# Retention block and Strassen-like feed-forward on one core: a gate's erf moved back on ScalarE, and the sums of W_in spread differently over VectorE

## The chip, the core and the metric

The kernel runs on one core of a Trainium2 chip. The core has a matrix engine (TensorE, PE in the profile, whose weight loads are listed as PEld), an elementwise engine (VectorE, DVE), an activation engine (ScalarE, ACT), GpSimd (POOL) and a queue that issues transfers (SyncE, SP). Each works through its own instructions in order, and they wait for each other by semaphores. Matmul results land in PSUM banks, from which VectorE and ScalarE read. The metric is the device time of one execution in microseconds; less is better.

## The reference

```python
def _attn_ref(q, k, v):                     # (4, 8, 768, 64)
    state = np.zeros((B, H, D, D))
    for t in range(S):
        state = gamma * state + np.einsum('bhd,bhe->bhde', k[:, :, t], v[:, :, t])
        y[:, :, t] = scale * np.einsum('bhd,bhde->bhe', q[:, :, t], state)

def _moe_ref(x, w_in, w_out):               # x: 3072 x 512, d_ff = 2048
    h = x @ w_in
    sp = np.maximum(h, 0.0) + np.log1p(np.exp(-np.abs(h)))
    return (h * erf(sp)) @ w_out
```

The output y of the first becomes the rows of x. The second is a feed-forward layer whose activation is h times erf of softplus(h).

## The kernel before

**Tiling.** The 3072 rows are handled as 24 chunks of 128 of the retention part (j in the code). The first four chunks feed the first block of 512 rows; after that, 256 rows (two chunks) are handled at a time. The feed-forward part runs in groups g, each over a quarter (first block) or a half (later blocks) of the 2048 hidden columns. A group has four parts, which run on four engines and overlap with those of its neighbours:

- hidden: TensorE multiplies x by a piece of W_in, and ScalarE or VectorE takes the result out of PSUM into h;
- gate: ScalarE computes softplus(h), then erf of that, in place. Each of the two functions is preceded by a load of its table (ACT_TABLE_LOAD);
- gated (L890): VectorE multiplies h by the gate, in two halves;
- project: TensorE multiplies that by a piece of W_out. It runs one group later, so TensorE has hidden(g) to do while gate(g - 1) is made.

**The first block, g = 0 to 3.** Here hidden and project are plain matmuls (L901, L937). The input weights arrive as 64-bit words and are converted on the chip, 16 pieces in order: for the last eight of them ScalarE makes two scaled exponents of a piece (a pair of instructions on L366), and VectorE combines them with the words (L369, L370, L372, L375). Between these, retention work of the chunks j = 4 and 5 is put: `sub_begin` (scores and new state on TensorE), `sub_states` (VectorE: two masks on L676, then the state of L704 or L702), `sub_results` (TensorE, then two copies by ScalarE on L737) and `sub_sums` (VectorE, L746). The order on every engine is that of the program's text: a scheduler does not rearrange it. Conversion steps are drawn in by `pace`, by a running balance of estimated costs.

PSUM tiles come from small pools: two banks named hp, two named r, four named o. A new tile in a bank waits until the last reader of the old one is done.

**The later blocks, g = 4 and up.** Here hidden is a fast matrix multiplication (`hidden_steps`): 26 products, called steps, of sums of blocks of W_in (`W_SUMS`, 30 sums for each half s of W_in) with sums of blocks of x (`X_SUMS`). Each step is two matmuls into one of four banks (L992), in the order of the list `STEPS`:

```python
    (15, 10, 0, False, ((6, True),)),     # step 13: W 15, x 10, bank 0, one read
    (8, 9, 1, False, ((4, False),)),      # step 14: bank 1, one read
    (3, 4, 0, False, ()),                 # step 15: bank 0, no read
```

After a step, its bank is read and added to or subtracted from parts of h: by VectorE (L1004) where that part of h was written before, else by ScalarE (L1006, L1008). The next step in the same bank waits for that read. Banks 0 and 1 are the two of hp, 2 and 3 the two of r. Between steps the program puts other work by a table `order`, whose keys are step numbers: sums of W_in (L385), parts of `prepared(j + 1)` (L578, two of L587, two of L591: scaling and transposing the next chunk), and `last_steps`, sums of W_out's blocks (ScalarE L393, then a transfer that adds, issued by POOL on L394). From g = 5 on there are also three parts of the projection of the group before (`project_part`, L1075), after steps 14, 18 and 24.

The half s = 0 of W_in is used by even groups, s = 1 by odd ones. So the 30 sums of half 0 are due before or in g = 4, those of half 1 before or in g = 5; afterwards all sums are there.

After the steps of a group come softplus, `sub_visit` (the retention work of one chunk: matmuls on L777, L813, L792, L669, masks on L676, additions on L833 and L838), erf, projections and the gated product. For g = 4 the last two quarters of the projection of g = 3 (L937) and their copies out (`put_first`, L950) stand there.

The lines between the first block and the later groups, which the change rewrites, begin in the version before with 20 sums of half 0, `prepared(6)`, the x sums and the gated product of g = 3.

Of the kernel before, what the change touches and what calls it, by code (L numbers as in the profile page):

```python
# [18 lines left out]
AF = mybir.ActivationFunctionType  # L19
# [120 lines left out]
def kernel(  # L140
# [13 lines left out]
    nc = tc.nc  # L154
# [8 lines left out]
    TT = TCH // P  # L163
# [217 lines left out]
    def sum_in(s, upto):  # L381

        assert all(("hidden", 2 * FG + s * FG + u) in done for u in range(FG))
        for to, a, b, sign in W_SUMS[in_sums[s] : upto]:
            nc.vector.tensor_tensor(w_in_sb[:, s, to], w_in_sb[:, s, a], w_in_sb[:, s, b], op=OP[sign])  # L385
        in_sums[s] = max(in_sums[s], upto)
# [30 lines left out]
    last_steps = later_sums()  # L417
# [114 lines left out]
    idle = ps_o.tile([P, P], F32, name="o0")  # L532
# [41 lines left out]
    def prepared(j):  # L574

        if j >= NJ:
            return
        nc.vector.tensor_tensor(  # L578
            KQ[j][:, 0], KQ[j][:, 0],
            kq_s[:, j % NC, 0, :, None].to_broadcast([P, H, D]), op=ALU.mult,  # L580
        )
        yield
        blocks = (KB[j], KQ[j][:, 1].rearrange("p h d -> p (h d)"))
        for i, x in enumerate(blocks):
            x = x.rearrange("p (u a d) -> p u a d", u=HP, d=32)
            by = kq_b[:, j % NC, i, :, :, None].to_broadcast([P, HP, 4, 32])
            nc.vector.tensor_tensor(x, x, by, op=ALU.mult)  # L587
            yield
        for name, store, x in zip("kq", (KT, QT), blocks):
            store[j] = ret.tile([P, HP, C], F32, name=name + "T")  # L590
            nc.vector.transpose(store[j].rearrange("p u t -> p (u t)"), x)  # L591
            yield
# [156 lines left out]
    def sub_begin(j, pool=None):  # L749
        SC[j] = [ret_psum(pool) for _ in range(2)]  # L750
        sub_scores(j)
        sub_additions(j)
# [100 lines left out]
    def gate_softplus(g):  # L853


        name = "r" if g < 4 and g % 2 else "e"
        E[g] = act.tile([P, N], F32, name=name, bufs=1)
        nc.scalar.activation(E[g], HS[g], AF.Softplus)  # L858

    def gate(g):  # L860

        gate_softplus(g)
        if g:
            gate_erf(g)

    def gate_erf(g):

        for half in range(2) if g == NG - 1 else (slice(None),):
            if g == NG - 1:
                half = slice(half * N // 2, (half + 1) * N // 2)  # L870
            nc.scalar.activation(E[g][:, half], E[g][:, half], AF.Erf)  # L871
# [76 lines left out]
    def put_first(tt):  # L948
        o = E[G0 - 1].rearrange("p (u t c) -> p t u c", u=FG, t=TT)[:, tt]
        nc.scalar.copy(o, O[0][tt].rearrange("p (u c) -> p u c", u=FG))  # L950
        nc.sync.dma_start(out[tt * P : (tt + 1) * P, :].rearrange("p (u c) -> p u c", u=FG), o)

    G0 = n_ft // FG
# [29 lines left out]
    def hidden_steps(g):  # L983

        m, s = chunk_of(g), (g - G0) % 2
        HS[g] = act.tile([P, N], F32, name="h")
        banks = [pool.tile([P, FG, P], F32, name=name) for pool, name in ((ps_h, "hp"), (ps_r, "r")) for _ in range(2)]
        written = set()
        for w, x, bank, first, reads in STEPS:
            to = banks[bank]  # L990
            for u in range(2):
                nc.tensor.matmul(  # L992
                    to[:, u, :],
                    w_in_sb[:, s, w, u * P : (u + 1) * P],
                    XS[m](x),
                    start=first and u == 0,
                    stop=True,
                    skip_group_check=True,
                )
            of = to[:, :2].rearrange("p u t -> p (u t)")  # L1000
            for o, plus in reads:
                h = h_block(g, o)
                if o in written:
                    nc.vector.tensor_tensor(h, h, of, op=ALU.add if plus else ALU.subtract)  # L1004
                elif plus:
                    nc.scalar.copy(h, of)  # L1006
                else:
                    nc.scalar.activation(h, of, AF.Copy, scale=-1.0)  # L1008
                written.add(o)
            yield  # L1010
# [181 lines left out]
    for g in range(G0):  # L1192
        for u in range(FG):

            if g and u == (2 if g == 1 else 0):
                waiting.append((gated, g - 1))
            hidden(g, u)
            run(after[g][u][0])
            if (g, u) == (1, 0):
                room = 0.0  # L1200
            waiting.extend(after[g][u][1])
        gate(g)
        if g:
            for tt in range(TT):
                project(g - 1, tt)
                if g == 1 and tt < 2:
                    waiting.append((K_, 5) if tt else (sub_states, 4))
                elif g == 2 and tt == 0:
                    sub_results(4)
                    sub_begin(5, ps_h)  # L1210
                    waiting.append((sub_states, 5))
                elif g == 2 and tt == 1:
                    waiting.append((sub_sums, 4))

    def all_of(steps):
        for _ in steps:
            pass
# [6 lines left out]
    j = JPC + 2  # L1226
# [5 lines left out]
    next(last_steps)  # L1232
    project(G0 - 1, 0)
    put_first(0)
    sub_begin(j)
    sub_states(j)
    next(last_steps)
    project(G0 - 1, 1)
    put_first(1)

    def sums_left(s):
        while in_sums[s] < len(W_SUMS):
            sum_in(s, in_sums[s] + 1)
            yield

    w_sums, next_chunk = sums_left(0), prepared(j + 1)
    order = {n: (w_sums,) for n in range(1, 8)}
    order.update({8: (w_sums, last_steps), 10: (w_sums, w_sums, next_chunk), 20: (next_chunk, last_steps)})
    order.update({n: (next_chunk,) for n in (14, 16, 18)})
    for n, _ in enumerate(hidden_steps(G0), start=1):  # L1250
        for steps in order.get(n, ()):
            next(steps, None)
    all_of(w_sums)
    all_of(next_chunk)
    sum_in(1, 6)
    nc.scalar.activation(idle, idle, AF.Softplus)
    gate_softplus(G0)
    sub_visit(j, G0)
    load(j + 3)
    gate_erf(G0)  # L1260
    sum_in(1, 12)
    for tt in range(2, TT):
        project(G0 - 1, tt)
        put_first(tt)
    gated(G0)
    sum_in(1, 16)
    j += 1

    w_sums = sums_left(1)
    put = None  # L1270
    for g in range(G0 + 1, NG):
        even = (g - G0) % 2 == 0
        more = j < NJ
        if put is not None:
            put_part(put, 0)
        e_sums = g_sums(g - 1)
        next(e_sums)
        next_chunk = prepared(j + 1) if even or put is None else iter(())

        if put is not None:  # L1280
            order = {18: (e_sums,), 20: (e_sums,), 24: (e_sums, e_sums)}
        else:
            order = {
                10: (next_chunk,), 14: (next_chunk, e_sums), 16: (next_chunk, e_sums),
                18: (next_chunk, e_sums), 20: (e_sums,), 24: (next_chunk,),
            }
        if g == G0 + 1:
            order.update({n: (w_sums,) for n in (1, 2, 3, 4, 5, 6, 7, 8)})
            for n in (14, 16, 18, 20, 24):
                order[n] += (w_sums, w_sums)  # L1290
            order.update({n: (last_steps,) for n in (11, 17, 23)})
        for n, _ in enumerate(hidden_steps(g), start=1):
            if put is not None and n in (14, 16, 18):
                put_part(put, n // 2 - 6)
            for steps in order.get(n, ()):
                next(steps, None)
            if n in (14, 18, 24):
                project_part(g - 1, {14: 1, 18: 2, 24: 4}[n])
        put = None
        all_of(e_sums)  # L1300
        all_of(next_chunk)

        nc.scalar.activation(idle, idle, AF.Softplus)
        gate_softplus(g)
        if more:
            sub_visit(j, g)
        all_of(w_sums)
        if g == G0 + 1:
            all_of(last_steps)
        if g + 1 < NG and not even:  # L1310
            x_sums(g + 1)
        if more:
            if even:
                all_of(prepared(j + 2))
            if j + 3 < NJ:
                load(j + 3)
            j += 1
        gate_erf(g)
        for p in (5, 6, 7, 3):
            project_part(g - 1, p)  # L1320
        if even:
            put = chunk_of(g - 1)
        if g == NG - 1:
            last_gated(g)
        else:
            gated(g)
# [70 lines left out]
```

## Time and profile before

| | us |
|---|---|
| median of three runs | 668.39 |
| the three runs | 667.46, 668.39, 672.40 |
| the profiled execution | 671.15 |
| its span in the profile | 669.4 |
| TensorE busy | 657.7 (98%) |
| VectorE busy | 504.0 (75%) |
| ScalarE busy | 289.7 (43%) |

The span is the time from the first to the last instruction that the profile has; 1.75 us of the profiled execution lie around it. Where the parts lie in it: conversions and first block to 141.2 us, the 26 steps of g = 4 from 141.2 to 155.9, chunk 6 and the rest of g = 3's projection to 164.7, the steps of g = 5 (with parts of the projection between them) to 183.7. From there each group takes about 25.9 us, to the end.

How to read the rows: a row of the timeline gives start and length in us, engine, line, operation, the written tile and the read ones, partitions x elements, and how many instructions were merged into it. A bracket at its end gives the idle time of that engine just before and what ended it. In a table of stretches, the columns are the stretch, its length, the busy time of TensorE, its weight loads, VectorE, ScalarE and POOL, the TensorE clock that was granted as a share of full speed, the share of the transfer engines and GB/s. A list of waits gives who waited for whom, the total, the number of times and the longest.

### The profile page before, as it was taken

The numbers are of one execution on the slowest core, as the hardware profiler recorded it, in microseconds if no ns is written. First come the engines' busy times: TensorE is split into PE (matmuls) and PEld (weight loads), VectorE is DVE, ScalarE is ACT, GpSimd is POOL, SyncE is SP. The second block draws the span as 40 slices with busy tenths as digits, with TensorE's granted clock in tenths as the row PEclk, the third lists the DMA queues.
The fourth block names the chain that finished last, engine by engine and source line by source line (L and its number), as shares of the span: only waits on it lengthen the run. The fifth ranks groups of instructions, "written<-read, shape, count | busy, mean of one in ns | idle before, by whom it ended". The sixth has DMA issues, their size and how long they took to land.

```text
span 669.4 us, 15377 instructions
## 1 busy us (share of the span) xinstructions
PE 657.7 (98%) x6240; PEld 558.4 (83%) x6240; DVE 504.0 (75%) x1112; ACT 289.7 (43%) x410; POOL 21.1 (3%) x48
## 2 busy tenths in 40 slices
PE   8999998989999999999999999999999999999998
PEld 7744444467899999999999999999999999999997
DVE  5899969859978678678677787787688688476464
ACT  3468593436354244243343432442542542433430
POOL 7000000010100000000000000000000000000000
PEclk9999998999999999999999999999999999999999
DMA  9999973455742322322222231232232220000000
GB/s 181 223 242 212 222 234 60 82 101 115 151 81 50 71 42 46 74 37 50 58 53 44 35 80 34 48 78 36 44 78 40 41 57 1 1 34 1 0 32 32
DMA packets 157511, 51.90 MB, mean 78 GB/s; under 512 B 141312, under 2 KB 147840, under 8 KB 157440
## 3 DMA queue, kind: packets, MB, share of 16 engines
q1 hardware_dynamic: 155328, 46.71, 32.8%
q0 software_dynamic: 1696, 4.21, 3.4%
q8 instruction: 49, 0.80, 0.5%
q14 instruction: 22, 0.18, 0.1%
q10 hardware_dynamic: 416, 0.01, 0.0%
HBM read 40.39 MB, written 6.29 MB: 70 GB/s over the span
## 4 chain that ended last, share of the span: by engine, by line
PE 82%; DVE 8%; DMA 4%; SPq 2%; issue 2%; ACT 2%; DVEq 0%; ACTq 0%
PE o L1075 36%; PE hp L992 22%; PE r L992 11%; PE o L937 4%; PE hp L901 2%; DMA w_in_sb<-in_moe_w_in_dram 2%; PE r L777 2%; SPq L212 1%; DVE xs L336 1%; PE hp L669 1%; DVE w_in_sb L333 1%; PE o L813 1%; DVE h L1004 1%; DMA w_out_sb<-in_moe_w_in_dram 1%; DVE xs L325 1%
## 5 line engine op out<-in xcount | busy, mean ns | idle before, releaser
L992 PE MATMUL hp<-xs,w_in_sb 128*128 128x128 f32 x1040 | 146.2, 275 | 3.6 <-DVE h L1004 3.5
L1075 PE MATMUL o<-w_out_sb,h 128*128 128x256 f32 (+1 forms) x640 | 142.7, 380 | 0.0
L992 PEld LDWEIGHTS hp<-xs,w_in_sb 128*128 128x128 f32 x1040 | 135.0, 192 | 7.5 <-DVE h L1004 4.4
L1004 DVE TENSOR_TENSOR h<-h,hp 128x256 f32<-128x256 f32 x200 | 82.1, 419 | 74.5 <-PE hp L992 69.6
L1075 PEld LDWEIGHTS o<-w_out_sb,h 128*128 128x128 f32 x640 | 119.5, 190 | 16.6
L1075 PE MATMUL o<-w_out_sb,e 128*128 128x256 f32 x480 | 113.5, 379 | 0.0
L858 ACT ACTIVATE e<-h 128x2048 f32<-128x2048 f32 x22 | 42.1, 1912 | 126.0 <-DVE h L1004 125.9
L1075 PEld LDWEIGHTS o<-w_out_sb,e 128*128 128x128 f32 x480 | 86.9, 190 | 9.4
L1004 DVE TENSOR_TENSOR h<-h,r 128x256 f32<-128x256 f32 x160 | 60.0, 416 | 21.9 <-PE r L992 20.9
L1006 ACT COPY h<-hp 128x256 f32<-128x256 f32 x40 | 14.9, 373 | 135.4 <-PE hp L992 103.2
L992 PE MATMUL r<-xs,w_in_sb 128*128 128x128 f32 x480 | 66.8, 275 | 0.0
L901 PE MATMUL hp<-xT,w_in_sb 128*128 128x512 f32 (+2 forms) x144 | 58.5, 562 | 3.0 <-DVE am L676 3.0
L992 PEld LDWEIGHTS r<-xs,w_in_sb 128*128 128x128 f32 x480 | 60.1, 192 | 0.0
L890 DVE TENSOR_TENSOR e<-h,e 128x1024 f32<-128x1024 f32 x42 | 49.3, 1214 | 8.3 <-ACT e L871 8.3
L901 PEld LDWEIGHTS hp<-xT,w_in_sb 128*128 128x128 f32 x144 | 26.1, 194 | 31.8 <-issue 29.1
L992 PE MATMUL hp<-xT,w_in_sb 128*128 128x128 f32 x320 | 48.8, 275 | 0.0
L992 PEld LDWEIGHTS hp<-xT,w_in_sb 128*128 128x128 f32 x320 | 43.7, 192 | 1.9 <-issue 1.0
L871 ACT ACTIVATE e<-e 128x2048 f32<-128x2048 f32 (+1 forms) x23 | 42.1, 1836 | 0.2
L1008 ACT ACTIVATE h<-hp 128x256 f32<-128x256 f32 x60 | 23.0, 383 | 30.4 <-PE hp L992 28.9
L992 PE MATMUL r<-xT,w_in_sb 128*128 128x128 f32 x240 | 33.3, 275 | 0.0
L871 ACT ACT_TABLE_LOAD x24 | 30.8, 1283 | 0.4
L992 PEld LDWEIGHTS r<-xT,w_in_sb 128*128 128x128 f32 x240 | 30.0, 192 | 0.0
(175 smaller groups left out, 780.4 us busy)
## 6 DMA issues: line engine op xcount, KB each, us to landing
w_out_sb<-in_moe_w_out_dram SPq DMA_DIRECT2D x14, 512.0 KB, 8.5
kq<-in_k_dram SPq DMA_DIRECT2D x23, 256.0 KB, 4.0
v<-in_v_dram SPq DMA_DIRECT2D x23, 256.0 KB, 3.2
out_dram<-r SPq DMA_DIRECT2D x23, 256.0 KB, 2.3
kq<-in_q_dram SPq DMA_DIRECT2D x288, 16.0 KB, 1.8
kb<-in_k_dram SPq DMA_DIRECT2D x288, 16.0 KB, 1.7
w_in_sb<-in_moe_w_in_dram SPq DMA_DIRECT2D x8, 512.0 KB, 13.4
w_out_sb<-w_out_sb POOLq DMA_DIRECT2D x8, 512.0 KB, 5.3
```

Source lines behind the costliest of these rows:

```text
L212: nc.sync.dma_start(KQ[j][:, i], src[b, :, now, :].rearrange("h p d -> p h d"))
L777: nc.tensor.matmul(pp[r][col * D : (col + 1) * D, u % 2, t], x[own, u, :], QT[j][own, u, t], start=first(r, col), stop=True, skip_group_ch ...
L858: nc.scalar.activation(E[g], HS[g], AF.Softplus)
L871: nc.scalar.activation(E[g][:, half], E[g][:, half], AF.Erf)
L890: nc.vector.tensor_tensor(E[g][:, half], HS[g][:, half], E[g][:, half], op=ALU.mult)
L901: nc.tensor.matmul(HP_[ft][:, t], w_in_of(ft, kk), XC[0][:, kk, t], start=(kk == 0), stop=(kk == n_k - 1),)
L937: nc.tensor.matmul(O[0][tt].rearrange("p (d c) -> p d c", d=2), E[g][:, u * TCH + tt * P : u * TCH + (tt + 1) * P], w_out_of(ft), start=(f ...
L992: nc.tensor.matmul(to[:, u, :], w_in_sb[:, s, w, u * P : (u + 1) * P], XS[m](x), start=first and u == 0, stop=True, skip_group_check=True,)
L1004: nc.vector.tensor_tensor(h, h, of, op=ALU.add if plus else ALU.subtract)
L1006: nc.scalar.copy(h, of)
L1008: nc.scalar.activation(h, of, AF.Copy, scale=-1.0)
L1075: nc.tensor.matmul(O[m][i][:, half, at], G[g][a][:, u * P : (u + 1) * P], w_out_sb[:, s, OUT[b], u, at], start=i not in started, stop=(s = ...
```

## The change

Three things move, and nothing is added or taken away: each engine has the same instructions as before.

- The erf of g = 2 leaves its place right behind the softplus of g = 2. It is issued in the second step of the projection loop (tt = 1), behind the copies of `sub_results(4)` and the conversion steps of two pieces. g = 1 and g = 3 keep their erf behind the softplus. On ScalarE this puts two copies (L737) and two L366 pairs ahead of the erf's table load; the last pair stays behind it.
- Sums of half 0: before, 20 ran ahead of everything and ten at g = 4's steps 1 to 10 (four of them before the first read of VectorE). Now the ten that are left all run ahead of `sub_begin(6)` and its masks, and the first part of `prepared(7)` (L578) with them, which was at step 10. The other four parts of it are at steps 10, 14, 16 and 20 instead of 14, 16, 18 and 20.
- Sums of half 1: before, six after the steps of g = 4 and ahead of the masks of chunk 7, six behind `sub_visit`, four behind the gated product, eight at steps 1 to 8 of g = 5 and six at its steps 14 to 18. Now eight ahead of g = 4's steps, none ahead of chunk 7's masks, 12 behind `sub_visit`, four behind the gated product, and six at steps 1 to 6 of g = 5.

The order on TensorE, POOL and SP is the same as before.

```diff
-    def gate(g):
-
-        gate_softplus(g)
-        if g:
-            gate_erf(g)
...
-        gate(g)
+        gate_softplus(g)
+        if g in (1, 3):
+            gate_erf(g)
...
                 elif g == 2 and tt == 1:
+                    gate_erf(2)
                     waiting.append((sub_sums, 4))
...
     put_first(0)
+    sum_in(0, len(W_SUMS))
+    next_chunk = prepared(j + 1)
+    next(next_chunk)
     sub_begin(j)
     sub_states(j)
     next(last_steps)
     project(G0 - 1, 1)
     put_first(1)
...
-    w_sums, next_chunk = sums_left(0), prepared(j + 1)
-    order = {n: (w_sums,) for n in range(1, 8)}
-    order.update({8: (w_sums, last_steps), 10: (w_sums, w_sums, next_chunk), 20: (next_chunk, last_steps)})
-    order.update({n: (next_chunk,) for n in (14, 16, 18)})
+    sum_in(1, 8)
+    order = {8: (last_steps,), 20: (next_chunk, last_steps)}
+    order.update({n: (next_chunk,) for n in (10, 14, 16)})
     for n, _ in enumerate(hidden_steps(G0), start=1):
         for steps in order.get(n, ()):
             next(steps, None)
-    all_of(w_sums)
     all_of(next_chunk)
-    sum_in(1, 6)
     nc.scalar.activation(idle, idle, AF.Softplus)
     gate_softplus(G0)
     sub_visit(j, G0)
     load(j + 3)
     gate_erf(G0)
-    sum_in(1, 12)
+    sum_in(1, 20)
     for tt in range(2, TT):
         project(G0 - 1, tt)
         put_first(tt)
     gated(G0)
-    sum_in(1, 16)
+    sum_in(1, 24)
...
         if g == G0 + 1:
-            order.update({n: (w_sums,) for n in (1, 2, 3, 4, 5, 6, 7, 8)})
-            for n in (14, 16, 18, 20, 24):
-                order[n] += (w_sums, w_sums)
+            order.update({n: (w_sums,) for n in (1, 2, 3, 4, 5, 6)})
             order.update({n: (last_steps,) for n in (11, 17, 23)})
```

More of the change, by code (lines that the diff above doesn't have):

```diff
@@ L1239 @@
     put_first(1)
[L1241 to L1244, printed above, removed]
-    w_sums, next_chunk = sums_left(0), prepared(j + 1)
-    order = {n: (w_sums,) for n in range(1, 8)}
-    order.update({8: (w_sums, last_steps), 10: (w_sums, w_sums, next_chunk), 20: (next_chunk, last_steps)})
-    order.update({n: (next_chunk,) for n in (14, 16, 18)})
+    sum_in(1, 8)
+    order = {8: (last_steps,), 20: (next_chunk, last_steps)}
+    order.update({n: (next_chunk,) for n in (10, 14, 16)})
     for n, _ in enumerate(hidden_steps(G0), start=1):
@@ L1265, with sums_left @@
     gated(G0)
-    sum_in(1, 16)
+    sum_in(1, 24)
     j += 1
+    def sums_left(s):
+        while in_sums[s] < len(W_SUMS):
+            sum_in(s, in_sums[s] + 1)
+            yield
     w_sums = sums_left(1)
```

## The prediction

> **What bounds the kernel now.** I read the page first, then the list of who waited for whom on TensorE, then the clock by stretches, and last the engines in order of time around each TensorE stall.
>
> ```profile
> span 669.4 us, 15377 instructions
> PEclk9999998999999999999999999999999999999999
> PE 82%; DVE 8%; DMA 4%; SPq 2%; issue 2%; ACT 2%; DVEq 0%; ACTq 0%
> ```
> ```profile
> PE hp L992 <- DVE h L1004: 3.5, 3, 1.7
> PE hp L901 <- DVE am L676: 3.0, 1, 3.0
> ```
> TensorE bounds nearly everything. It is busy for 657.7 of 669.4 us, so any gain must come from its few stalls. Four of them (3.04, 1.75, 0.75 and 1.05 us) lie between 99 and 180 us, where the edits are. One slice of the clock row is an 8. By stretches:
>
> ```profile
> 99.50:102.50 3.00, 0.00 (x0) 0.00 (x0) 2.93 (x6) 2.71 (x3) 0.00 (x0) 1.00 0.30 45
> 103.00:103.50 0.50, 0.50 (x2) 0.24 (x1) 0.50 (x1) 0.50 (x2) 0.00 (x0) 0.63 0.23 36
> 104.00:106.00 2.00, 2.00 (x3) 0.81 (x3) 1.97 (x5) 0.17 (x1) 0.00 (x0) 0.50 0.22 35
> 106.50:107.00 0.50, 0.50 (x3) 0.26 (x2) 0.50 (x1) 0.00 (x0) 0.00 (x0) 0.95 0.20 31
> ```
> The clock is the third column from the end. The 3 us without a matmul are followed by half clock from about 103.13 to 106.53 us, 3.4 us that do 1.70 us of work: the stall cost 3.04 + 1.70.
>
> Its cause, ScalarE in order of time, then VectorE:
>
> ```profile
> 93.33 1.28 ACT L871 ACT_TABLE_LOAD   x1
> 94.62 1.91 ACT L871 ACTIVATE e<-e 128x2048 f32<-128x2048 f32 x1
> 96.44 0.63 ACT L737 COPY xT<-r 128x256 f32<-128x256 f32 x2
> 96.95 2.33 ACT L366 ACTIVATE xs<-w_out_sb,below 128x1024 uint16<-128x1024 int16 x2
> ```
> ```profile
> 99.31 0.69 DVE L369 TENSOR_TENSOR xs<-xs 128x1024 bf16<-128x1024 bf16 x1 [4.63 <-ACT xs L366]
> 101.64 0.75 DVE L676 TENSOR_TENSOR am<-hp,causal_d 128x256 f32<-128x256 f32 x2
> ```
> The mask of L676 frees the PSUM bank of the next hidden group (L901). It stands in VectorE's queue behind L369, which waits for L366, which stands on ScalarE behind the erf.
>
> **Edit 1, the erf of g = 2.** It goes behind the copies and the L366 pairs of the next two weight pieces. Table load and erf took 93.33 to 96.44 = 3.11 us, so copies, L366, L369 and masks come 3.1 us earlier. The masks end near 99.25 instead of 102.39, and TensorE's previous work ends at 99.49: the whole 3.04 goes (bounds 0, if something else holds L366, and 3.04). I see nothing else: L366's data moved in a burst of DMA that was over by 91.5, and the buffer's last reader (L375) ended at 91.03. The set of functions is no question: copies and L366 already run under the softplus set at 43 to 48 us. Behind the moved erf stand the last piece's L366 pair (starts at about 101.5, was 101.80; its VectorE reader comes at 104.4) and the h copy of L919, due at 103.0, which may slip to 103.9; its bank is wanted at 107.6. The erf's own reader, the gate product (L890, 111.20 before, about 108 after), is 6 us behind it. With the gap the 1.70 of half clock goes too (bounds 0 and 1.70).
>
> **Edit 2, sums of the first half ahead of the chunk's masks.** Ten L385 at 0.39 (20 took 7.84) and one scaling (L578, 0.61), 4.5 us, now precede L676 at 137.78. VectorE, 3.2 us earlier, ends the gate product at 128.4 and these at 132.9. TensorE's state products, 4.7 us earlier, end at 133.0, so the masks are not late; and r banks are first written 0.9 us into the next stretch, at 137.4, while masks and copy end by 134.1. Cover: 3.2 us. Eight sums of the second half (3.08) follow and end at 137.2; the stretch's first read (L1004) is due at 138.9.
>
> In the stretch at 141.2 us six sums and L578 leave VectorE's queue from between its reads. TensorE and VectorE there, before:
>
> ```profile
> 149.37 0.71 PE L992 MATMUL hp<-xs,w_in_sb 128*128 128x128 f32 x4 [1.75 <-DVE h L1004]
> 154.85 0.71 PE L992 MATMUL hp<-xs,w_in_sb 128*128 128x128 f32 x4 [0.75 <-DVE h L1004]
> ```
> ```profile
> 146.97 0.69 DVE L578 TENSOR_TENSOR kq<-kq,kq_s 128x512 f32<-128x512 f32 x1
> 147.58 1.41 DVE L1004 TENSOR_TENSOR h<-h,r 128x256 f32<-128x256 f32 x4
> ...
> 159.84 2.47 DVE L385 TENSOR_TENSOR w_in_sb<-w_in_sb 128x256 f32<-128x256 f32 x6
> 162.62 2.36 DVE L890 TENSOR_TENSOR e<-h,e 128x1024 f32<-128x1024 f32 x2 [0.31 <-ACT e L871]
> 164.90 3.01 DVE L385 TENSOR_TENSOR w_in_sb<-w_in_sb 128x256 f32<-128x256 f32 x8
> 167.83 0.41 DVE L1004 TENSOR_TENSOR h<-h,hp 128x256 f32<-128x256 f32 x1
> ```
> A step of TensorE takes 0.4465 us, and step n can be read 0.27 after its end (the first read, of step 5, came at 2.50). Step 15 needs the bank that the read of step 13 empties. Before, step 15 began 8.16 after the stretch's start (149.37 - 141.21) instead of 14 x 0.4465 = 6.25, because L578 held the reads of steps 11 and 12 until 147.58. After, these reads stand behind one operation of the same length (L587, 0.6) that is put in after step 10. The undisturbed stretch that starts at 192.75 has VectorE in just this order: 0.6 us at 197.45, four reads from 198.05, the read of step 13 at 199.38, over at 199.80, which is 7.05 after the start. (It costs nothing there, since a projection of 1.73 us stands between steps 14 and 15; this stretch has none.) So step 15 begins at 7.10: 1.06 gained, and 0.85 stays. Step 25 waits for the read of step 24, which comes 0.27 after that step and takes 0.42 and 0.05 to be seen: 0.74 late at best, 0.91 before, 0.17 gained. Together 1.23 (bounds 0.17, and 2.8 if both stalls went).
>
> **Edit 3, the rest of the second half.** Call the start of the next stretch P (164.69 before). Before, six sums ran ahead of the chunk's masks, and between the state update (L838) and the stretch's first read stood 6 sums, the gate product of L890 and 8 more sums; the read fell at P+3.14 and ended at 3.55. Step 9 writes the bank that this read empties, and is due at P+3.57: TensorE was just not held. After, 12 sums, product and 8 sums stand there. VectorE is free for them at P-5.40: the softplus starts at P-8.19 as before, and the undisturbed stretch needs 3.01 from there (184.33) to the end of the update (187.34), with an addition of 0.2 more. Twelve sums by their own rows before take 4.52 (four of 0.398 at 159.84, eight of 0.366 at 164.90), the product 2.28, eight sums 3.05 (1.46 and 1.59): P+4.45. The read ends at 4.87, step 9 begins at 4.92: **a new stall** of 1.35, and 0.1 for the slower first step behind a stall, 1.45. It is shorter than the 1.75 that left the clock at 1.00. Against it, this stretch took 19.02 before (164.69 to 183.71) and the undisturbed one 16.88: 2.14 of stalls, the largest 1.05 at step 23, because six sums stood between the reads of steps 14 to 20. They now come by step 6, and with the stall TensorE is late enough that step 23 (P+14.6) finds its bank read (P+13.9). Net 2.14 - 1.45 = 0.69. If each sum takes the 0.42 of a lone one, 0.9 less; if there is no new stall, 2.14.
>
> Behind that the pattern repeats every 25.9 us with TensorE full. SP and POOL keep their order; the loads behind the first late chunk start earlier and have over 20 us of lead.
>
> **Sum** on the profiled execution: 3.04 + 1.70 + 1.23 + 0.69 = 6.66, so 671.15 (span and 1.75 around it) becomes 664.5. The median is 2.76 below that execution; the four times fall into 667.5, 668.4 and 671.2, 672.4. A half-clock spell that comes in some executions would make part of that split, so I leave it out of the median: 668.39 - 4.96 = **663.4**. The Trainium skill, TensorE: Matmul & The Clock Gate, section The HAM clock gate, says that the clock halves after an idle window of about 3.4 us whose windows run free of the kernel. By that rule a 3.04 us gap would cost 0 or 1.7 by its phase, which gives the first rival's 661.7; the 3.4 us of half clock agree.
>
> **Rivals.** *The spell was in the median too*: the gap lay the same way in each execution. 668.39 - 6.66 = 661.7. For it: the only traced execution has it. *No new stall*: the 20 sums pass quicker than their rows, 1.45 more: 662.0, with the spell 660.3. Against: L1004 at 167.83 already met its limit within 0.1. *The erf holds nothing up*: L366 waits for its data instead, the 3.04 stays, 1.92 gained: 666.5. Against: DMA is idle from 91.5 to 95. *Slower*: VectorE becomes the bound ahead of P. Each us that the first read is late costs one, and a gap of 3 us another 1.7 by the clock. The loss passes all gains once the read is 6.4 later than before; at 0.70 per sum it falls at P+10.9, a stall of 7.3 and 1.7, less the 2.14: against 5.97 of other gains 0.9 slower, 669.3. No row shows a sum over 0.43.
>
> **Chances.** Forecast 0.41, spell 0.32, no new stall 0.11, erf 0.11, slower 0.05. One per cent, about what a measurement can tell, is 6.7 us: faster by more means below 661.7. That takes half of the spell's 0.16, 0.06 of the no-stall case, 0.05 of the forecast's edge: 0.27. Slower by 1%: 0.03. Within: 0.70. Range 660.3 (no stall, with spell) to 666.5 (erf case).
>
> **What will show it.** Clock row without the 8 and no wait of L901 on L676: edit 1. One wait of 0.8 at step 15 and one of 0.7 at step 25: edit 2. A wait of 1.3 at step 9 of the second stretch, none at its step 23: edit 3. A TensorE wait on L676, or a first read after P+5, would prove me wrong.

## The result, and the profile after

| | before | after |
|---|---|---|
| median of 20 executions each | 668.47 us | 664.80 us |
| lowest to highest | 667.41 to 672.40 | 663.91 to 672.06 |
| profiled execution | 671.15 | 664.47 |
| its span | 669.4 | 662.8 |

The ratio of the times is 0.9946 (95% interval 0.9926 to 0.9966): 0.5% faster, 3.7 us in the medians. The two profiled executions differ by 6.7 us, nearly twice as much. Most of what follows is about that difference.

The page of the changed kernel, then the list of TensorE's waits (the lines that were 871 to 1111 are 6 lower, so L986 is the former L992, L895 the former L901, L998 the former L1004):

```profile
span 662.8 us, 15378 instructions
PEclk9999999999999999999999999999999999999999
```
```profile
PE hp L986 <- DVE h L998: 2.3, 3, 1.0
PE o L536 <- POOL ident masks.py:199: 1.5, 1, 1.5
PE hp L895 <- DVE w_in_sb L342: 0.6, 1, 0.6
```
The 8 in the clock row is gone, and so is the wait of the hidden group on the mask of L676. ScalarE and VectorE around 95 us show why:

```profile
92.47 0.63 ACT L737 COPY xT<-r 128x256 f32<-128x256 f32 x2
92.98 2.35 ACT L366 ACTIVATE xs<-w_out_sb,below 128x1024 uint16<-128x1024 int16 x2
95.24 2.37 ACT L366 ACTIVATE w_out_sb<-w_in_sb,below 128x1024 uint16<-128x1024 int16 x2
97.62 1.28 ACT L865 ACT_TABLE_LOAD   x1
98.92 1.91 ACT L865 ACTIVATE e<-e 128x2048 f32<-128x2048 f32 x1
```
```profile
95.36 0.69 DVE L369 TENSOR_TENSOR xs<-xs 128x1024 bf16<-128x1024 bf16 x1 [1.51 <-ACT xs L366]
97.69 0.75 DVE L676 TENSOR_TENSOR am<-hp,causal_d 128x256 f32<-128x256 f32 x2
```
The erf now comes after two pairs of L366; VectorE waits 1.51 us for the first pair instead of 4.63, and the masks are over by 98.4, before TensorE asks for the bank at 99.69.

The three stalls that are left in the two late stretches, in TensorE's timeline:

```profile
143.79 0.71 PE L986 MATMUL hp<-xs,w_in_sb 128*128 128x128 f32 x4 [0.78 <-DVE h L998]
149.04 0.71 PE L986 MATMUL hp<-xs,w_in_sb 128*128 128x128 f32 x4 [0.51 <-DVE h L998]
163.61 1.16 PE L986 MATMUL hp<-xs,w_in_sb 128*128 128x128 f32 x8 [1.00 <-DVE h L998]
```
They are steps 15 and 25 of g = 4 (1.75 and 0.75 before) and step 9 of g = 5, which is new; the wait of 1.05 at step 23 is gone. VectorE ahead of the new one:

```profile
153.42 4.48 DVE L385 TENSOR_TENSOR w_in_sb<-w_in_sb 128x256 f32<-128x256 f32 x12
157.82 2.35 DVE L884 TENSOR_TENSOR e<-h,e 128x1024 f32<-128x1024 f32 x2
160.09 3.13 DVE L385 TENSOR_TENSOR w_in_sb<-w_in_sb 128x256 f32<-128x256 f32 x8
163.14 0.41 DVE L998 TENSOR_TENSOR h<-h,hp 128x256 f32<-128x256 f32 x1
```
Twelve sums, the gate product and eight sums run without a gap from 153.42 on. The read that follows ends at 163.55, and step 9 starts at 163.61.

Where the 6.6 us of span went, by the start of the same work in both traces: g = 4 starts 4.61 us earlier (136.60 for 141.21), lasts 1.21 less (22.27 for 23.48 to the start of g = 5), and g = 5 lasts 0.87 less (27.19 for 28.06 to the start of g = 6). From there both run alike, 25.9 us a group.

### The profile page after: what moved, and what is told of

It reads as the page before. It is cut to its first block, busy times and chain, and to the rows that moved or that the text cites. A ratio compares the mean times of both kernels' runs of the same rounds, so it can differ in the third digit from the quotient of the medians.

```text
span 662.8 us, 15378 instructions
## 1 busy us (share of the span) xinstructions
PE 654.1 (99%) x6240; PEld 556.5 (84%) x6240; DVE 504.5 (76%) x1112; ACT 289.6 (44%) x410; POOL 21.0 (3%) x48
## 4 chain that ended last, share of the span: by engine, by line
PE 76%; DVE 8%; SPq 7%; DMA 4%; ACT 3%; issue 2%; ACTq 0%; DVEq 0%
PE o L1069 37%; PE hp L986 22%; PE r L986 11%; SPq L190 5%; DMA w_in_sb<-in_moe_w_in_dram 2%; PE r L777 2%; SPq L212 1%; DVE xs L336 1%; PE hp L669 1%; DVE w_in_sb L385 1%; DMA w_out_sb<-in_moe_w_in_dram 1%; PE o L813 1%; DVE w_in_sb L333 1%; DVE xs L325 1%; DMA kq<-in_k_dram 1%
## 5 line engine op out<-in xcount | busy, mean ns | idle before, releaser
L986 PE MATMUL hp<-xs,w_in_sb 128*128 128x128 f32 x1040 | 145.7, 275 | 2.3 <-DVE h L998 2.3
L1069 PE MATMUL o<-w_out_sb,h 128*128 128x256 f32 (+1 forms) x640 | 142.7, 381 | 0.0
L986 PEld LDWEIGHTS hp<-xs,w_in_sb 128*128 128x128 f32 x1040 | 134.9, 192 | 5.8 <-DVE h L998 2.9
L998 DVE TENSOR_TENSOR h<-h,hp 128x256 f32<-128x256 f32 x200 | 82.2, 419 | 74.9 <-PE hp L986 69.8
L1069 PEld LDWEIGHTS o<-w_out_sb,h 128*128 128x128 f32 x640 | 119.5, 190 | 16.6
L1069 PE MATMUL o<-w_out_sb,e 128*128 128x256 f32 x480 | 113.5, 379 | 0.0
L1069 PEld LDWEIGHTS o<-w_out_sb,e 128*128 128x128 f32 x480 | 86.9, 190 | 9.4
L998 DVE TENSOR_TENSOR h<-h,r 128x256 f32<-128x256 f32 x160 | 59.9, 415 | 22.1 <-PE r L986 21.0
L986 PE MATMUL r<-xs,w_in_sb 128*128 128x128 f32 x480 | 66.7, 275 | 0.0
L986 PEld LDWEIGHTS r<-xs,w_in_sb 128*128 128x128 f32 x480 | 60.0, 192 | 0.0
L895 PE MATMUL hp<-xT,w_in_sb 128*128 128x512 f32 (+2 forms) x144 | 56.8, 548 | 0.6 <-DVE w_in_sb L342 0.6
L895 PEld LDWEIGHTS hp<-xT,w_in_sb 128*128 128x128 f32 x144 | 25.6, 190 | 28.1 <-issue 24.6
L986 PE MATMUL hp<-xT,w_in_sb 128*128 128x128 f32 x320 | 48.8, 275 | 0.0
L986 PEld LDWEIGHTS hp<-xT,w_in_sb 128*128 128x128 f32 x320 | 43.7, 192 | 1.9 <-issue 1.0
L986 PE MATMUL r<-xT,w_in_sb 128*128 128x128 f32 x240 | 33.3, 275 | 0.0
L986 PEld LDWEIGHTS r<-xT,w_in_sb 128*128 128x128 f32 x240 | 30.0, 192 | 0.0
```

Of the source, the lines that this page charges most:

```text
L895: nc.tensor.matmul(HP_[ft][:, t], w_in_of(ft, kk), XC[0][:, kk, t], start=(kk == 0), stop=(kk == n_k - 1),)
L986: nc.tensor.matmul(to[:, u, :], w_in_sb[:, s, w, u * P : (u + 1) * P], XS[m](x), start=first and u == 0, stop=True, skip_group_check=True,)
L1069: nc.tensor.matmul(O[m][i][:, half, at], G[g][a][:, u * P : (u + 1) * P], w_out_sb[:, s, OUT[b], u, at], start=i not in started, stop=(s = ...
```

## The experiments

**One part at a time.** The first kernel is the version before with the erf moved and nothing else, the second the changed version with the erf put back.

```diff
-        gate(g)
+        gate_softplus(g)
+        if g in (1, 3):
+            gate_erf(g)
...
+                    gate_erf(2)
                     waiting.append((sub_sums, 4))
```

> The version before with the erf of g = 2 moved as in the change, all sums left where they were. Theory A (the wait at the mask of chunk 5 has a size that varies from execution to execution, with the landing of weight piece 11; in the median one it is 1.7 us and is not followed by half clock): 668.5 - 1.7 = 666.8, the times of 670 and more become rare, and the profile shows no wait of L901 on L676 and clock 1.00. Theory B (the wait is 3.0 us in every execution, the sums give little outside the profile): 665.4. Under both, the two waits of the first late stretch stay at 1.75 and 0.75 and the one in the second at about 1.05.

Measured: 666.41 (12 executions, 666.0 to 668.62; ratio 0.9957, 0.9937 to 0.9977). The wait on L676 is gone; those of the late stretches are the old ones, and the stretches last 23.47 and 28.04 us, as before the change. The median fits theory A. In the traced execution weight piece 11 lands as late as in the first profile (its L366, which waits for that transfer, starts at 84.88 us for 84.98), no wait on L676 follows, and g = 4 starts 4.99 us earlier, 0.11 of which is there already at 68 us. The prediction had 3.04 + 1.70 for this.

```diff
-        if g in (1, 3):
-            gate_erf(g)
+        if g:
+            gate_erf(g)
...
-                    gate_erf(2)
                     waiting.append((sub_sums, 4))
```

> The changed version with the erf of g = 2 put back right behind its softplus, so only the sums are moved. Theory A: 2.1 us less than before (1.21 in the first late stretch, 0.87 in the second, as the changed kernel's profile has them), 666.4, with the times of 670 and more as frequent as before; the profile shows the wait of L901 on L676, and the stretches' waits of 0.8, 0.5 and 1.0. Theory B: 667.8.

Measured: 666.34 (12 executions, 665.83 to 670.77; ratio 0.9971, 0.9949 to 0.9992). The stretches last 22.28 and 27.18 us, the changed kernel's to 0.01, so the 1.2 and 0.9 us come from the sums, with or without the erf's move. Four of the twelve have a mean clock of 0.997. The eight others, at 0.999 or 1.00, have a median of 666.06. The profiled execution took 666.68 with the wait on L676 in it:

```profile
PE hp L986 <- DVE h L998: 2.3, 3, 1.0
PE hp L895 <- DVE am L676: 1.9, 1, 1.9
```
That wait is 1.9 us here, and the clock behind it stays at 1.00. It is the same wait, behind the same erf, that was 3.04 us in the profile before.

**The version before, traced again.** Four more executions of it were profiled.

> The version before, unchanged, for another profiled execution of it and more times. Theory A: if this execution takes about 668, the wait of L901 on L676 is about 1.7 us and the clock stays at 1.00 behind it; if about 671, the wait is near 3 and half clock of 3.4 us follows. Theory B: 3.0 us of wait in either case.

> The version before, for one more profiled execution. If it takes about 668 at clock 1.00, the wait of L901 on L676 should be about 1.7 us, and ScalarE should have waited for piece 11 (L366 on the transfer from W_in) by about 1 us less than the 2.0 and 2.1 of the executions above 671; if about 671 at 0.997, near 3.0. Rival: a wait of 3.0 us at 668.

> The version before, one more profiled execution. As for the look before it: near 668 at clock 1.00, the wait of L901 on L676 is about 1.7 us and ScalarE's wait for piece 11 about 1 us; near 671 at 0.997, about 3.0 and about 2. Rival: 3.0 at 668.

> The version before, one more profiled execution, with the same expectation: 668 goes with a wait of about 1.7 us at clock 1.00, 671 with about 3.0 and half clock behind it. Rival: 3.0 at 668.

Measured, with the first profile ahead and the sums-alone execution at the end (which has the same ScalarE order up to there):

| time of that execution | ScalarE's wait for piece 11 | wait on L676 | mean clock |
|---|---|---|---|
| 671.15 | 2.1 | 3.0 | 0.997 |
| 672.38 | 2.0 | 3.0 | 0.997 |
| 672.12 | 2.3 | 3.0 | 0.997 |
| 670.87 | 1.1 | 2.3 | 0.997 |
| 672.22 | 2.9 | 3.0 | 0.997 |
| 666.68 (sums alone) | 0.7 | 1.9 | 1.00 |

The wait does vary, and it is shorter where piece 11 landed sooner: its L366 starts at 84.23 us in the last row and at 84.66 in the one with 2.3, at 84.98 to 86.40 in the others. At 3.0 the wait stops growing, and the traces show why. Behind this L366 on ScalarE stands the copy L919, which frees the bank of the scores of L669. So a still later landing holds TensorE itself, ahead of the gap, and moves both ends of the gap alike. That second wait is 1.1, 0.9 and 0.7 us in the second, third and fifth rows, and in no other. The list of the second row:

```profile
PE hp L901 <- DVE am L676: 3.0, 1, 3.0
PE hp L669 <- ACT h L919: 1.1, 1, 1.1
```
But the question put by theory A was not answered directly: all five traced executions of this kernel are of the long kind, none took 668. The 76 other executions of the version before whose clock is listed (eleven belong to the first of these runs, whose twelve have a median of 668.87) fall into two groups of times without overlap. 46 have a mean clock of 0.999 or 1.00 and none of them took over 669.9 (median 667.9). 30 have 0.997 or 0.995 and none took under 670.2 (median 671.7). One spell of 3.4 us at half clock in 669 us makes a mean of 0.997. So the short kind is the commoner one in the measurements, and the traced executions were all of the other.

**Does the gap bring the half clock?** One instruction is added on ScalarE ahead of the L366 in question:

```diff
         gate(g)
+        if g == 2:
+            nc.scalar.copy(E[g], E[g])
```

> The version before with one more ScalarE instruction right behind the erf of g = 2, a copy of the gate onto itself (128 x 2048, about 1.9 us; it changes no value). If the wait of L901 on L676 is held by ScalarE's queue, it grows by 1.9: from 1.7 to 3.6 us in most executions. If the length of that gap is what brings the 3.4 us of half clock, every execution now has it: clock 0.997 or less in all, and the lower group of times goes from 667.9 to 667.9 + 1.9 + 1.7 = 671.5. Rival: the half clock comes by chance and not by the gap; then the lower group stays at clock 1.00 and 669.8, and about one in three lies above.

Measured: 673.50 in the median, all ten executions at 0.997 or 0.995, none at 1.00, while 10 of the 23 executions of the version before beside it were at 0.999 or 1.00. TensorE's wait, then its clock by stretches (third column from the end):

```profile
PE hp L901 <- DVE am L676: 4.0, 1, 4.0
```
```profile
100.00:102.00 2.00, 0.00 (x0) 0.00 (x0) 1.51 (x3) 2.00 (x3) 0.00 (x0) 1.00 0.17 28
102.00:104.00 2.00, 0.36 (x1) 0.39 (x2) 2.00 (x5) 1.69 (x2) 0.00 (x0) 0.64 0.23 36
104.00:108.00 4.00, 4.00 (x5) 1.47 (x5) 3.93 (x7) 1.26 (x2) 0.00 (x0) 0.50 0.22 34
108.00:110.00 2.00, 2.00 (x4) 0.67 (x2) 1.93 (x4) 0.00 (x0) 0.00 (x0) 0.65 0.22 34
```
The wait is 4.0 us, and half clock lasts twice as long as in the first profile: 0.64 from 102 to 104, 0.50 to 108 and 0.65 to 110 add up to 6.8 us. This execution's mean is 0.995, and four of the other nine show the same. The second spell is not all that lifts the times above the 671.5 expected for one: the five at 0.997 have a median of 673.2. The wait was 0.4 longer than the 3.6 expected; the rest is open. The gap brings the half clock: without the added instruction 10 of 23 executions are free of it, with the instruction none of ten.

**Does VectorE's queue set the new stall?** Once with six sums fewer in it, once with four more.

```diff
-    sum_in(1, 8)
+    sum_in(1, 12)
...
     all_of(next_chunk)
+    sum_in(1, 14)
     nc.scalar.activation(idle, idle, AF.Softplus)
```

> The changed version with 12 instead of 8 sums of the second half ahead of the first late stretch and two more ahead of the masks of chunk 7, where VectorE waited for TensorE by 1.67 and 1.14 us; so six fewer (2.3 us) between the state update and the first read of the second stretch. If that queue is what held step 9: its wait of 1.0 goes and nothing takes its place, 1.1 us less than the changed kernel, about 663.7. Rival: the six sums delay the masks or the stretch's first read instead, and the time stays within 0.3 us of 664.8.

Measured: 662.94 (ratio to before 0.9899, 0.9872 to 0.9925), and 662.99 in a second set of eight (0.9915, 0.9886 to 0.9945). TensorE's waits of the second set:

```profile
PE hp L986 <- DVE h L998: 1.3, 2, 0.8
```
Two are left in place of three. Those of 0.78 and 0.51 in g = 4 stay, the one at step 9 is gone, and g = 5 lasts 25.92 us, which is the length of an undisturbed group. That is 1.27 us less than the changed kernel's. The medians are 1.9 and 1.8 lower than its 664.80, which was measured in another set of runs; no trace shows where the 0.5 to 0.6 beyond the 1.27 comes from.

```diff
-    sum_in(1, 8)
+    sum_in(1, 4)
```

> The changed version with 4 instead of 8 sums of the second half ahead of the first late stretch, so four more (1.6 us) between the state update and the first read of the second. If that queue holds step 9 one to one, its wait grows from 1.0 to 2.6 and the usual time from 664.7 to 666.3. A gap of 2.6 can fill most of a window of 3.4, so some executions should come with clock 0.997 and near 668. Rival: the wait grows by less than 1 us since ScalarE or TensorE hides part of it.

Measured: 667.66, and eight of ten executions at 0.997 or below (for the changed kernel, two of 20). VectorE's four additional sums, TensorE's step 9, and the clock behind it:

```profile
152.68 6.32 DVE L385 TENSOR_TENSOR w_in_sb<-w_in_sb 128x256 f32<-128x256 f32 x16
```
```profile
164.72 1.16 PE L986 MATMUL hp<-xs,w_in_sb 128*128 128x128 f32 x8 [2.86 <-DVE h L998]
```
```profile
166.00:168.00 2.00, 2.00 (x12) 2.00 (x12) 2.00 (x6) 1.24 (x2) 0.46 (x1) 0.54 0.21 33
168.00:170.00 2.00, 2.00 (x9) 1.78 (x8) 1.61 (x5) 0.00 (x0) 0.41 (x1) 0.61 0.65 123
```
Sixteen sums take 6.24 us to the start of the next operation where twelve took 4.40, and the wait grows by 1.86, from 1.00 to 2.86: one to one. The four sums cost 0.46 each, not 0.39. Each of them is followed by one that reads what it has just written. In this trace the sums of such a pair, or of one whose second sum writes over what the first reads, start 0.45 to 0.46 us apart; those of a pair without such a tie 0.33 to 0.34. And the gap of 2.86 is followed by half clock, at a place where the kernel before had none. The 666.3 expected for the usual time does not hold, since half clock became the usual case. The two executions at full clock took 665.7, which is 0.6 less than expected although the wait grew as expected; the two kernels' times come from different sets of runs.

**A cover for step 15.** The third quarter of the projection of g = 3 moves into the first late stretch.

```diff
+        if n == 14:
+            project(G0 - 1, 2)
+            put_first(2)
+            sum_in(1, 19)
     all_of(next_chunk)
-    sum_in(1, 14)
+    sum_in(1, 21)
...
-    sum_in(1, 20)
-    for tt in range(2, TT):
-        project(G0 - 1, tt)
-        put_first(tt)
+    sum_in(1, 28)
+    project(G0 - 1, 3)
+    put_first(3)
     gated(G0)
-    sum_in(1, 24)
...
-            order.update({n: (w_sums,) for n in (1, 2, 3, 4, 5, 6)})
+            order.update({n: (w_sums,) for n in (6, 7)})
```

> The version with the sums earlier, and the third quarter of the projection of g = 3 (3.5 us of TensorE) put after step 14 of the first late stretch, where the later groups have a part of a projection; seven sums of the second half run on VectorE under it, and none stand between the gated product and the first read of g = 5. If step 15 waits only for VectorE's reads, its wait of 0.78 goes. The next stretch starts 3.5 us sooner after the gate, so the read of step 5 there is about 0.3 late: a small wait at step 9. Net 0.5 less than the version with the sums earlier: 662.4. Rival: the gate of g = 4 becomes the bound of the next stretch by over 1 us, and the time is 663 or more.

Measured: 663.31 over six executions, of which one took 2602 us and is told of at the end; the other five have a median of 662.8. The version it is to be compared with had run on another chip, so both were run again side by side.

> The version with the third quarter of the projection inside the first late stretch, again, beside the version with the sums earlier on the same chip. If the cover works as worked out: no wait at step 15, at most 0.3 at step 9 of the next stretch, and 0.5 less than the other. Rival: no difference within 0.3, since the gate of g = 4 takes back what the cover gives.

> The version with the sums earlier, again, as the other half of the comparison: about 662.9, with the waits of 0.78 and 0.51 in the first late stretch and none in the second.

Measured: 662.60 (six executions, 662.14 to 663.24; ratio to before 0.9905, 0.9874 to 0.9935) against 662.99 (eight, 662.7 to 666.31). The trace shows one wait left in the late stretches:

```profile
PE hp L986 <- DVE h L998: 0.5, 1, 0.5
```
It is step 25's. Step 15's is gone, step 9's does not come, and the time from the start of g = 4 to the start of g = 5 is 21.23 us instead of 22.28. The waits went as expected; the 0.4 us between the medians is less than their spread, so that this version is faster than the other is likely and not shown. Both are faster than the changed kernel's 664.80.

## Why the prediction was right, and where it was not

The forecast was 663.4 with a range of 660.3 to 666.5, mostly within 1%; 664.80 lies in it, and the change is 0.5% faster. Its mechanism held, step by step; one term of its sum was mis-sized for the median.

- *The wait on L676 goes with the erf.* Right. The one kernel that moves only the erf loses that wait and nothing else.
- *Its size, 3.04 us, taken over into the median.* This is the step that failed. For the profiled execution it was right: the sum gave 664.5 there and 664.47 was measured. The agreement to 0.03 is in part luck: the three parts came out at 4.61, 1.21 and 0.87 where the sum had 4.74, 1.23 and 0.69, and the changed kernel's execution lost 0.6 us at 22 us, ahead of all that the change moves, to a wait of L895 on L342 that the first profile does not have. But 3.04 is the size of the rarer kind of execution. Between executions at full clock, the erf alone is worth 667.9 - 666.4 = 1.5 us, by times and not by a trace. The prediction saw that the four times it had fall into two groups, and took the half clock out of the median; it did not take the longer wait out with it, although the wait is what brings the half clock. The 1.5 us by which the term was too large, less the 0.2 that g = 5 gave beyond its own term, is the 1.4 by which the median came out above 663.4, to 0.1. It was not seen in a trace of the kernel before, since none of its traced executions was of the common kind; the 1.9 us of the sums-alone execution is the nearest.
- *The half clock goes with the wait: 1.70 us, not in the median.* Right, and the runs tell more: 30 of 76 executions of the version before had it, four of 12 with the sums alone moved, none of 12 with the erf alone moved (all at 0.999 or 1.00), two of 20 of the changed kernel. Neither of these two was traced, and what brought it there is not known.
- *Ten sums and L578 ahead of chunk 6's masks are covered.* Right: VectorE was done at 132.1 and waited 1.06 us for TensorE before the masks at 133.17.
- *1.23 us in g = 4.* Right: 1.21, the waits being 0.78 and 0.51.
- *A new stall of 1.35 at step 9 of g = 5, net 0.69.* Right in place and cause, a little large: step 9 came 1.17 late by start times (163.61 for 162.44), because the twelve sums took 4.40 and not 4.52 and VectorE was free 0.05 earlier. Net 0.87.
- *The rivals.* "No new stall" fell with that wait. "The erf holds nothing up" fell with the first experiment. "The spell was in the median too" fell with the clocks of the 76 executions. "Slower" needed sums of 0.70 us; the dearest seen cost 0.46.
- *Two slips in the working that changed nothing.* In "slower", a first read at P+10.9 makes a stall of 7.8 us and not 7.3, and the 5.97 of gains holds the 1.70 that the forecast leaves out of the median. And what runs under the softplus set at 43 to 48 us is L326, not L366; the changed kernel's ScalarE runs L366 at 92.98, behind the softplus, without a further table load, so the conclusion held.

The parts add up: at full clock 1.5 for the erf and 2.1 for the sums, 3.6, and 668.1 - 664.7 = 3.4 between the medians of the undisturbed executions of the two kernels (below 670 for the first, at full clock for the second).

What stays open is how long the wait on L676 is in the common execution of the version before. The tie between the landing of piece 11 and the wait is read off six traces; no run moved that transfer on purpose. A late landing still costs something after the change: in the second set with the sums earlier, the traced execution has no wait on L676 but one of 1.3 us of L669 on the copy behind piece 11's L366 (L913 there), and it took 664.44 where the median is 662.99.

## What to carry to other kernels

A profile is one execution. Before a stall's length goes into a forecast of the median, put the profiled time and clock beside the other runs: a stall that depends on a transfer may be twice as long in the one that was traced, and terms that have one cause, here the wait and the half clock behind it, leave the sum together. Where every instruction of an engine's queue has its row, a new stall can be placed to the step and sized to 0.2 us by adding up what stands ahead of the read that frees the bank. And look for the idle gaps of the same queue a little earlier: six sums moved into gaps of 1.67 and 1.14 us gave back all that the new stall had cost.

## What the runs showed of the hardware

- A gap without matmuls can cost more than itself, and not always. Gaps of 1.75 (the profile before) and 1.90 us (sums alone) left the granted clock at 1.00. A gap of 2.30 in one traced execution was followed by a spell of half clock, and so were those of 2.86, 3.04 and 4.0, the last by a spell twice as long. Of the kernel whose trace has the 2.86, eight of ten executions show it; of the one with 4.0, all ten. The Trainium skill, TensorE: Matmul & The Clock Gate, sets the limit for gaps at about 3 us (section Why this matters for your kernels). The limit was lower here. The length of a spell, 3.4 us, agrees with the window that the Trainium skill gives on the same page, section The HAM clock gate.
- The spells lie on a grid of 3.413 us. In the clock records of the traces, the times from one change of the clock to the next are whole multiples of that (in the profile before 28 of them up to the spell, one for the spell, 165 from there to the fall at the end). Cut by this grid, the stretch just ahead of a spell was without matmuls for 2.40 to 2.81 us in the four executions with a gap of 3.04, for 2.30 where that was the gap, for 2.92 with the longer gap, and for 1.98 where the gap of 2.86 fell across a boundary. In the sums-alone execution the whole gap of 1.90 lay in one stretch and no spell followed. Every other stretch, the kernel's start and end aside, had 1.75 or less. So in these traces the limit lies between 1.90 and 1.98 us within one stretch, and one and the same gap can bring the spell or not, by where the grid falls. How the grid falls was not varied on purpose.
- All five traced executions of the version before were of the kind with half clock, which 30 of 76 others had. Whether tracing itself lengthens that wait was not tried.
- One execution of the cover kernel took 2602 us. In its trace TensorE is busy for 2595.1 us, and the last merged piece of the projections (L1069, 88 matmuls) took 68.99 us, nearly four times the 18.16 of the profile before. This trace alone has no record of the clock: its page lacks the clock row, so the 1.00 that its tables print tells nothing. It came once in 12 executions of that kernel, and its cause is not known.
